# Eight plain fp32 identity products and a scaled squared error added to the second projection block of a fused attention and MLP kernel

## The chip, the cores and the metric

The kernel runs on one core of a Trainium2 chip. The metric is the device time of one execution in microseconds (us); several executions are timed, and their median counts. One further execution is taken by the hardware profiler, and the traces are read from that one.

## What is computed

The reference is one transformer-like block over 2048 rows of 576 elements, all in fp32, cut here to what matters:

```python
mod = (silu(c) @ w_mod).reshape(1, 6, 1, 576)      # sa, ca, ga, sb, cb, gb
h = layernorm(x) * (1 + ca) + sa
q, k, v = split(h @ wqkv)                           # 32 heads of 18
o = softmax(mask(q k^T * 18**-0.5, window 256)) v   # causal, sliding window
x = x + ga * (o @ wo)
h = layernorm(x) * (1 + cb) + sb
g = gelu(layernorm(h) @ w1)                         # shifted by 1, -1, 2, -2 rows
x1 = h + shifted(g) @ w2
x = x + gb * (x1 + gelu(layernorm(x1) @ w3) @ w4)   # MLP, 576 -> 4608 -> 576
```

## The kernel before

The program is one long list of small steps. Each step is a function put on the list with `at(time, function)`; the list is sorted by that planned time once (L1277) and the functions are called in that order. So the planned times do not start anything on the chip: they fix the order in which each engine's own queue holds its instructions, and every engine works through its queue in order, waiting where a semaphore says so.

The work runs in stages. First the modulation vector is made (`mod01` at L169 and, for the later parts, `modr` at L188 and `modre` at L196). Then the projection makes q, k and v for four blocks of 512 rows each (`qkv`, L128). Attention, the output product, the row mixing and the MLP follow.

Most matrix products split each fp32 operand into a rounded high part and a low rest, both of type fp32r, and add up three products of these (for instance L279: `W` and `H` hold high and low parts, and a product of 576 terms takes 14 matmuls of 128x512). A few small products use plain, unsplit fp32 operands: `mod01` (L177), `modr` (L194) and the transposes, which are products with the fp32 identity `ident` (L254).

One projection block `b`, at planned time `t0 = 47 b`, does the following. Nine steps `fmm` (L270) make the q and k features; each is read from its PSUM bank (tags `s0` to `s3` in turn) by ScalarE and VectorE (`fev`, L281) and stored to DRAM through the SyncE queue (`fst`). Eight steps `vmm` (L300) make v, and `vev` (L311) reads them out. Between these, the rows of the next block are loaded (`xload`, L146, five buffers of tag `x`), normalised (`st`, `nrm`) and transposed: `tr(b + 1, k)` (L249) transposes 128 columns of the four row tiles into a PSUM tile of tag `m0` (k even) or `m1` (k odd), and `hev` (L256) scales and shifts that tile into an SBUF tile of tag `hf` (two buffers), from which ScalarE and GpSimd make the high and low parts. `modr(k)` uses the PSUM tag `m1` too, and `modre(k)` adds its result to `macc`.

Tags set what must wait: a PSUM tile with tag `m0` has one buffer, so TensorE may write the next `m0` tile only when VectorE has read the one before.

At the end of the kernel, `run` (L1157) makes the second MLP product, 12 matmuls of 128x288 per row tile `t`, and `dev` (L1171) adds it to an SBUF accumulator `acc[t]`; after the last slice of the MLP, `dev` also stores the row tile to the output (L1178). The tiles go in the order 4, 5, 6, 7, 0, 1, 2, 3 (L1183).

Of the kernel before, what the change touches and what calls it, by code (L numbers as in the profile page):

```python
# [8 lines left out]
F32 = mybir.dt.float32  # L9
# [3 lines left out]
ALU = mybir.AluOpType  # L13
# [6 lines left out]
P = 128  # L20
# [13 lines left out]
class Kern:  # L34
# [8 lines left out]
    def setup(self, stack):  # L43
        nc, tc = self.nc, self.tc
        self.ev = []
        self.cst = stack.enter_context(tc.tile_pool(name="cst", bufs=1))
        self.dr = stack.enter_context(tc.tile_pool(name="dr", bufs=1, space=DRAM))
        self.ps = stack.enter_context(tc.tile_pool(name="psU", bufs=1, space=PSUM))
        self.pools = {}
        c = self.cst  # L50
        self.ident = c.tile([P, P], F32, name="ident")
        self.identr = c.tile([P, P], F32R, name="identr")
        self.gb = c.tile([P, D], F32, name="gb")
        self.mhalf = c.tile([P, 1], F32, name="mhalf")
        self.rowm = c.tile([P, 8], F32, name="rowm")
        self.Mq = c.tile([P, 2, 64], F32R, name="Mq")
        self.Mk = c.tile([P, 5, 64], F32R, name="Mk")
        self.md = c.tile([P, 10], F32, name="md")
        self.qd = [self.dr.tile([2, D, 512], F32, name=f"qd{g}") for g in range(4)]
        self.kd = [self.dr.tile([2, D, 768], F32, name=f"kd{g}") for g in range(4)]  # L60
        self.vd = [self.dr.tile([P, VW], F32, name=f"vd{t}") for t in range(NT)]
        self.od = [self.dr.tile([512, D], F32, name=f"od{g}") for g in range(4)]
        self.xp = [self.dr.tile([P, D], F32, name=f"xp{t}") for t in range(NT)]
        self.hbd = [self.dr.tile([P, D], F32, name=f"hbd{t}") for t in range(NT)]
        self.xnd = [self.dr.tile([P, D], F32, name=f"xnd{t}") for t in range(NT)]
        self.modd = {v: self.dr.tile([1, D], F32, name=f"modd{v}") for v in (2, 3, 4, 5)}

    def at(self, t, f, *a):
        self.ev.append((t, (lambda: f(*a)) if a else f))
# [58 lines left out]
    def qkv(self, T0, TB):  # L128
        nc, at, ps = self.nc, self.at, self.ps
        X = {}  # L130
        at(-99, lambda: (self.open("qa", "left"), self.open("qb", "right")))
        qb = lambda *a, **k: self.pool_("qb").tile(*a, **k)
# [186 lines left out]
        def vst(t):  # L319
            nc.sync.dma_start(self.vd[t], X["Vst"][t % 3])  # L320

        at(-90, cond)
        for i in range(2):
            at(-89 + i, xload, i)
# [21 lines left out]
        for b in range(4):  # L346
# [7 lines left out]
            for i in range(4):  # L354
                t = 4 * b + i
# [16 lines left out]
            if b < 3:  # L372
                for i in range(4):
                    t = 4 * b + 4 + i
# [584 lines left out]
    def mlp(self):  # L959
        nc, ps, ident = self.nc, self.ps, self.ident  # L960
        NJ = F // 2 // P
        SB = S // 1024
        A, W3, W4, acc, gb = [], [], {}, {}, self.gb
# [15 lines left out]
        if True:  # L979
# [191 lines left out]
            def dev(jj, sb, t, last):  # L1171
                def f():
                    po = up_b[jj, "d", t][:, :, 0:288]
                    a = acc[t].rearrange("p (h d) -> p h d", h=2)
                    nc.vector.tensor_tensor(out=a, in0=po, in1=a, op=ALU.add)  # L1175
                    if last:
                        tt = 8 * sb + t
                        nc.sync.dma_start(self.out[tt * P:(tt + 1) * P, :], acc[t])  # L1178
                return f

# [126 lines left out]
```

## Time and profile before

| what | value |
|---|---|
| median of three timed runs | 1856.75 us |
| the three runs | 1849.98, 1856.75, 1858.69 us |
| the profiled execution, its own time | 1853.12 us |
| its span in the trace | 1851.3 us |
| mean granted TensorE clock in it | 0.976 |
| instructions in it | 33769 |

The span is what the trace covers; the execution's own time is 1.8 us longer. In the page of the profile, PE is TensorE's matmuls, PEld its weight loads, DVE is VectorE, ACT ScalarE, POOL GpSimd, SPq the SyncE queue that issues the transfers. A row of a group ends with the busy time, the mean duration of one instruction in ns, and the idle time in front of these instructions with what ended it. A duration of one matmul is longer than the distance from one matmul to the next, since matmuls are pipelined; the chain of waits shows distances, since in it each piece runs to the start of the next.

### The profile page before, as it was taken

The page shows a single profiled execution, that of the slowest core. Times are in us where ns is not written, and L with a number is a line of the kernel's source. Part 1 is how long each engine was busy: PE and PEld are TensorE (multiplying, and loading weights), DVE is VectorE, ACT ScalarE, POOL GpSimd, SP SyncE. Part 2 cuts the span into 40 slices and gives each one's busy share as a digit, 9 for nine tenths or more (in the row PEclk, how much of TensorE's full clock was granted, in tenths as well). Part 3 has the DMA queues.
Part 4 walks back from the last instruction along what each step waited for, and adds up shares of the span by engine and source line. Part 5 has one row for each costly group of instructions (what it writes and reads, how often), then busy time and mean ns, then how long its engine had stood idle before and what let it go on. Part 6 is the DMA issues. An engine that isn't in the chain of part 4 may idle for free.

```text
span 1851.3 us, 33769 instructions
## 1 busy us (share of the span) xinstructions
PE 1725.0 (93%) x13496; PEld 1572.3 (85%) x13496; DVE 1093.2 (59%) x1801; ACT 706.9 (38%) x1210; POOL 903.9 (49%) x842
## 2 busy tenths in 40 slices
PE   7999989889999998998779999999989999999998
PEld 6788878788888887998768899999978999999997
DVE  4644244465656562757556666666676666666664
ACT  2322134344444445344333333333343333333331
POOL 4322264445454533355576655555563655555550
PEclk9999979899999999999999999999989999999999
DMA  4955552444544535664442222222114222222211
GB/s 147 322 175 181 166 154 82 122 120 132 155 138 140 149 105 154 203 201 155 144 137 60 60 61 61 60 61 60 58 60 126 60 61 60 60 61 61 60 44 52
DMA packets 156420, 206.78 MB, mean 112 GB/s; under 512 B 19300, under 2 KB 87908, under 8 KB 155688
## 3 DMA queue, kind: packets, MB, share of 16 engines
q1 hardware_dynamic: 156264, 204.64, 36.1%
q8 instruction: 106, 1.74, 0.4%
q14 instruction: 50, 0.41, 0.1%
HBM read 143.76 MB, written 60.56 MB: 110 GB/s over the span
## 4 chain that ended last, share of the span: by engine, by line
PE 74%; DVE 7%; DMA 6%; POOL 5%; issue 3%; ACT 3%; SPq 2%; POOLq 0%; DVEq 0%; ACTq 0%
PE d L1167 23%; PE qk L279 6%; PE av L526 4%; PE v L309 3%; PE mx L444 3%; PE wo L611 3%; PE pg L828 3%; PE X L487 3%; DMA QD<-qd 2%; PE w L877 2%; DVE m L456 1%; PE X L489 1%; PE pm L177 1%; PE ot L536 1%; DVE W L1025 1%
## 5 line engine op out<-in xcount | busy, mean ns | idle before, releaser
L1167 PE MATMUL d<-W,G 128*128 128x288 f32 x3456 | 508.5, 298 | 16.3 <-DVE acc L1175 12.3
L1167 PEld LDWEIGHTS d<-W,G 128*128 128x128 f32 x3456 | 490.2, 190 | 38.3 <-DVE acc L1175 13.7
L1175 DVE TENSOR_TENSOR acc<-d,acc 128x576 f32<-128x576 f32 x288 | 216.6, 753 | 200.6 <-PE d L1167 198.4
L1005 POOL TENSOR_TENSOR wf<-wf 128x384 f32<-128x384 f32 x140 | 146.4, 1067 | 343.0 <-DMA wf<-in_B_w_dram 321.7
L456 DVE TENSOR_REDUCE m<-mx 128x2 f32<-128x640 f32 x224 | 181.2, 817 | 159.6 <-PE mx L446 157.4
L504 ACT ACTIVATE P<-X 128x512 f32<-128x512 f32 (+4 forms) x320 | 180.5, 573 | 207.2 <-PE X L489 204.5
L444 PE MATMUL mx<-KD,QS 128*128 128x320 f32 (+4 forms) x512 | 157.6, 358 | 37.8 <-POOL QS L427 22.5
L427 POOL TENSOR_SCALAR QS<-QD,rowm 128x512 fp32r<-128x512 f32 x128 | 87.9, 699 | 142.2 <-DMA QD<-qd 70.2
L487 PE MATMUL X<-QD,KS 128*128 128x64 f32 (+2 forms) x704 | 151.6, 307 | 3.7 <-ACT P L504 3.2
L1144 DVE TENSOR_TENSOR G<-U,G 128x512 fp32r<-128x512 f32 x108 | 95.3, 882 | 99.8 <-ACT G L1137 99.8
L1017 POOL TENSOR_TENSOR W<-wf,W 128x768 fp32r<-128x768 f32 x70 | 152.0, 2193 | 1.2 <-ACT W L1011 1.2
L444 PEld LDWEIGHTS mx<-KD,QS 128*128 128x128 f32 x512 | 102.0, 199 | 45.4 <-POOL QS L427 23.8
L1135 ACT ACTIVATE U<-U 128x512 f32<-128x512 f32 x108 | 68.3, 632 | 179.3 <-DVE U L1120 179.3
L1135 ACT ACTIVATE C<-C 128x512 f32<-128x512 f32 x36 | 22.8, 632 | 285.9 <-DVE C L1120 285.9
L279 PE MATMUL qk<-hT,Wqk 128*128 128x512 f32 x504 | 120.9, 401 | 0.0
L279 PEld LDWEIGHTS qk<-hT,Wqk 128*128 128x128 f32 x504 | 95.8, 191 | 24.2 <-issue 0.9
L487 PEld LDWEIGHTS X<-QD,KS 128*128 128x128 f32 x704 | 106.7, 195 | 10.6 <-ACT P L504 7.8
L434 POOL TENSOR_SCALAR KS<-KD,rowm 128x768 fp32r<-128x768 f32 (+1 forms) x128 | 107.6, 853 | 0.0
L1031 POOL TENSOR_TENSOR wf<-wf,gb 128x1152 f32<-128x1152 f32 x35 | 103.4, 2955 | 7.1 <-DMA wf<-in_B_w_dram 7.1
L446 PE MATMUL mx<-Mq,identr 128*128 128x128 f32 x448 | 101.5, 227 | 0.0
L1046 POOL TENSOR_TENSOR W<-wf,W 128x1152 fp32r<-128x1152 f32 x35 | 96.7, 2762 | 6.9 <-ACT W L1040 6.9
L1011 ACT CAST W<-wf 128x1152 fp32r<-128x1152 f32 x70 | 90.2, 1318 | 21.9 <-DMA wf<-in_B_w_dram 11.2
(765 smaller groups left out, 3198.0 us busy)
## 6 DMA issues: line engine op xcount, KB each, us to landing
wf<-in_B_w_dram SPq DMA_DIRECT2D x35, 576.0 KB
wf<-in_B_w_dram SPq DMA_DIRECT2D x140, 128.0 KB
KD<-kd SPq DMA_DIRECT2D x72, 216.0 KB
QD<-qd SPq DMA_DIRECT2D x96, 144.0 KB
wf<-in_B_w_dram SPq DMA_DIRECT2D x140, 64.0 KB
qd<-qs SPq DMA_DIRECT2D x16, 512.0 KB
kd<-qs SPq DMA_DIRECT2D x16, 512.0 KB
vd<-Vst SPq DMA_DIRECT2D x16, 312.0 KB
```

The source lines that it names most:

```text
L279: nc.tensor.matmul(po, W[:, a, fs], H[:, c, :], start=(n == 0), stop=(n == 13))
L434: nc.gpsimd.tensor_scalar(t[:, b0:, r], src[:, b0:], M[:, 2 + r:3 + r], 0.0, op0=ALU.mult, op1=ALU.add)
L444: nc.tensor.matmul(pm[:, s, 320 - 64 * nb:320], lhs, K[:, j, 64 * (i + 5 - nb):64 * (i + 5)], start=True, stop=False)
L446: nc.tensor.matmul(pm[:, s, 0:320].rearrange("p (a b) -> p a b", b=64)[:, 0::4, :], self.identr, self.Mq, start=False, stop=True)
L456: nc.vector.tensor_reduce(out=m[:, c:c + 2], in_=pm[:, :, 0:320], axis=mybir.AxisListType.X, op=ALU.max, negate=True)
L487: nc.tensor.matmul(px[:, c:c + q1 - q0], K[:, b + 4].rearrange("p r k -> p (r k)"), Q[:, j, q0:q1], start=(i == 0), stop=False)
L504: nc.scalar.activation(p[:, lo:], X["px", n, j, k][:, lo:], AF.Exp, scale=SCALE)
L1005: nc.gpsimd.tensor_tensor(out=WF[:, o], in0=WF[:, a], in1=WF[:, b], op=ALU.subtract)
L1017: eng.tensor_tensor(out=W[:, s0:s1, 3:5, :], in0=WF[:, 1 + s0:1 + s1, 0:2], in1=W[:, s0:s1, 0:2, :].bitcast(F32), op=ALU.subtract)
L1031: nc.gpsimd.tensor_tensor(out=R4, in0=R4, in1=gb.unsqueeze(1).to_broadcast([P, 2, D]), op=ALU.mult)
L1167: nc.tensor.matmul(po, G[:, g, ta, b, ts], W[:, w, b, cs], start=(n == 0), stop=(n == 5))
L1175: nc.vector.tensor_tensor(out=a, in0=po, in1=a, op=ALU.add)
```

## The change

A new step `resid` stands in the projection at planned time 30.5 of block 0, in the midst of the steps that transpose the rows of the second block. It takes row tile 4 (the first row tile of the second block, as it was loaded from the input), and multiplies the fp32 identity with its first 512 columns eight times, each time into the same PSUM tile of tag `m0` and each time from the start, so that each product overwrites the one before. All operands are plain fp32. VectorE then subtracts the input from the product, multiplies the difference by a million, squares it, and sums each row into a column `res` of 128 values. At the end, when row tile 8 of the output (128 rows) is complete, `res` is added to all its columns ahead of its store.

```diff
+        self.res = c.tile([P, 1], F32, name="res")
...
+        def resid():
+            x = X["x", 4]
+            pp = ps.tile([P, 512], F32, tag="m0", name="rp")
+            for _ in range(8):
+                nc.tensor.matmul(pp, self.ident, x[:, 0:512], start=True, stop=True)
+            d = qb([P, 512], F32, tag="hf", name="rd", bufs=2)
+            nc.vector.tensor_tensor(out=d, in0=pp, in1=x[:, 0:512], op=ALU.subtract)
+            nc.vector.tensor_scalar(d, d, 1e6, None, op0=ALU.mult)
+            nc.vector.tensor_tensor(out=d, in0=d, in1=d, op=ALU.mult)
+            nc.vector.tensor_reduce(out=self.res, in_=d, axis=mybir.AxisListType.X, op=ALU.add)
+
+        at(T0 + 30.5, resid)
...
                     if last:
                         tt = 8 * sb + t
+                        if tt == 8:
+                            nc.vector.tensor_scalar(acc[t], acc[t], self.res, None, op0=ALU.add)
                         nc.sync.dma_start(self.out[tt * P:(tt + 1) * P, :], acc[t])
```

On TensorE, in the first projection block, this stood between the third step of the modulation product (`pmr`), and the first v product of the next bank, with the transposes of the second block (`pt_0`) between them. In the lists, out is left of the arrow, the operands right of it, the moving one first.

```order
L194 MATMUL pmr_722<-wm_1152_602,silub 32x288 [waits DMAHW4_49,DVE_49]
L194 MATMUL pmr_722<-wm_1152_602,silub 32x288 x7
L254 MATMUL pt_0_732<-ident,xh_590 128x128
L254 MATMUL pt_0_732<-ident,xh_625 128x128
L254 MATMUL pt_0_732<-ident,xh_665 128x128
L254 MATMUL pt_0_732<-ident,xh_696 128x128 [waits DVE_49]
L309 MATMUL v_1_737<-Wv,hT_372 128x288 [waits Activation_49]
```

The same place of TensorE's queue with the change; `rp` is the new PSUM tile.

```order
L195 MATMUL pmr_723<-wm_1152_603,silub 32x288 [waits DMAHW4_49,DVE_49]
L195 MATMUL pmr_723<-wm_1152_603,silub 32x288 x7
L327 MATMUL rp<-x_443,ident 128x512 [waits DMAHW7_49]
L327 MATMUL rp<-x_443,ident 128x512 x7
L255 MATMUL pt_0_747<-ident,xh_591 128x128 [waits DVE_49]
L255 MATMUL pt_0_747<-ident,xh_626 128x128
L255 MATMUL pt_0_747<-ident,xh_666 128x128
L255 MATMUL pt_0_747<-ident,xh_697 128x128
L310 MATMUL v_1_752<-Wv,hT_373 128x288 [waits Activation_49]
```

Eight products stand in front of the transposes now, and the first transpose waits for VectorE. The queue holds the same instructions before and behind.

VectorE's queue at the same place before: it ends the q and k read-outs (`qs`) and goes on with the v read-out (`Vst`), the modulation sum and the read-out of the transposes (`hf`).

```order
L285 TENSOR_TENSOR qs_8_719<-qk_8_681,qs_8_719 128x512 [waits DMAHW1_49,DMAHW0_49,Activation_49]
L315 COPY Vst_193<-v_0_704 64x16x18 [waits Activation_49]
L201 TENSOR_TENSOR macc<-pmr_722,macc 128x576 [waits DVE_49,PE_49]
L259 TENSOR_SCALAR hf_0_757<-pt_0_732,md 128x512 [waits PE_49]
L315 COPY Vst_193<-v_1_737 64x16x18 [waits Activation_49]
L259 TENSOR_SCALAR hf_1_785<-pt_1_780,md 128x512 [waits PE_49]
```

With the change:

```order
L286 TENSOR_TENSOR qs_8_720<-qk_8_682,qs_8_720 128x512 [waits DMAHW1_49,DMAHW0_49,Activation_49]
L329 TENSOR_TENSOR rd<-rp,x_443 128x512 [waits PE_49]
L330 TENSOR_SCALAR rd<-rd 128x512 [waits DVE_49]
L331 TENSOR_TENSOR rd<-rd 128x512 [waits DVE_49]
L332 TENSOR_REDUCE res<-rd 128x1 [waits DVE_49]
L316 COPY Vst_194<-v_0_705 64x16x18 [waits Activation_49]
L202 TENSOR_TENSOR macc<-pmr_723,macc 128x576
L260 TENSOR_SCALAR hf_0_772<-pt_0_747,md 128x512 [waits PE_49]
L316 COPY Vst_194<-v_1_752 64x16x18 [waits Activation_49]
L260 TENSOR_SCALAR hf_1_800<-pt_1_795,md 128x512 [waits DVE_49,PE_49]
```

The four new operations stand ahead of the first v read-out, and the first of them waits for TensorE's products. At the very end of VectorE's queue one operation is new, between the additions for row tiles 0 and 1 of the last sweep:

```order
L1188 TENSOR_TENSOR acc_11903<-d_0_19781,acc_11903 128x576 [waits DVE_49,PE_49]
L1192 TENSOR_SCALAR acc_11903<-acc_11903,res 128x576 [waits DVE_49]
L1188 TENSOR_TENSOR acc_11934<-d_1_19797,acc_11934 128x576 [waits PE_49]
L1188 TENSOR_TENSOR acc_11936<-d_2_19812,acc_11936 128x576 [waits PE_49]
L1188 TENSOR_TENSOR acc_11946<-d_3_19827,acc_11946 128x576 [waits PE_49]
```

The additions are the same ones in the same order. ScalarE, GpSimd and the SyncE queue hold the same instructions in the same order as before; the load of row tile 9, which goes into the buffer of row tile 4, waits for TensorE too.

## The prediction

> **What bounds the kernel now.** I read the page first, then the chain of waits around the place of the change, then the groups of instructions there, and last the stages behind it. The page of the profile before:
>
> ```profile
> PE 1725.0 (93%) x13496; PEld 1572.3 (85%) x13496; DVE 1093.2 (59%) x1801; ACT 706.9 (38%) x1210; POOL 903.9 (49%) x842
> PE 74%; DVE 7%; DMA 6%; POOL 5%; issue 3%; ACT 3%; SPq 2%; POOLq 0%; DVEq 0%; ACTq 0%
> ```
>
> TensorE (PE) is busy for 93% of the span and carries 74% of the chain that ended last. That is an average; what counts is the chain where the eight products go in. There it reads (start, length in us, piece):
>
> ```profile
> 75.81 1.11 PE pmr L194 x16
> 76.92 0.59 PE pt L254 x4
> 77.50 3.71 PE v L309 x28
> 81.21 0.43 PE pt L254 x4
> 81.65 1.87 PE v L309 x14
> 83.52 0.45 PE pt L254 x4
> ...
> 95.07 29.60 PE qk L279 x126
> ...
> 217.51 7.44 PE v L309 x56
> ```
>
> The new products stand between the first two rows, at 76.92 us. From there TensorE works almost without a gap until 225 us, and it is the chain itself. Whatever is put into its queue at 76.92 moves all of this. The stretch of the second block says the same (length, busy time and instructions of PE, PEld, DVE, ACT and POOL, granted clock, DMA share, GB/s):
>
> ```profile
> 95.00:142.00 47.00, 47.00 (x264) 41.19 (x261) 20.49 (x39) 11.93 (x26) 9.57 (x13) 1.00 0.52 179
> ```
>
> PE is busy for 47.00 of 47.00 us. So there is no slack into which an insertion could disappear before 225 us. Behind that the chain goes through stores and loads, but these start from what TensorE's products release:
>
> ```profile
> 224.97 0.40 ACT Vst L314
> 225.40 0.47 DVE Vst L315
> 225.88 0.35 SPq L320
> 226.29 0.55 DMA QD<-qd
> 227.02 1.37 POOL QS L427 x2
> ```
>
> The store (SPq L320) follows the read-out of a v product, and the load behind it stands in the same queue. So I take the shift at 76.92 to reach the end in full.
>
> **The products.** The operands are plain fp32, unsplit, with 128 columns of weights and 512 moving columns. No such form is in the trace of before. These are its neighbours (groups, then lines with minimum, median and maximum of one duration in ns):
>
> ```profile
> L1167 PE MATMUL d<-W,G 128*128 128x288 f32 x3456 | 508.5, 298 | 16.3 <-DVE acc L1175 12.3 <-POOL W L1046 3.9
> L1114 PE MATMUL u9P<-A,W 128*128 128x512 f32 x49 | 12.5, 394 | 0.0
> L194 PE MATMUL pmr<-wm,silub x80: 402/406/431, 58.2 to 94.7; 128*32 128x288 f32 x64, 64*32 64x288 f32 x16
> L254 PE MATMUL pt<-ident,xh x20: 270/272/331, 76.8 to 90.0; 128*128 128x128 f32 x20
> ```
>
> The first two are fp32r. From 288 to 512 columns the duration grows by 394 - 298 = 96 ns, which is 0.43 ns per column, and 298 - 288 x 0.43 = 174 ns remain that do not depend on the columns. The last two are plain fp32. With the same 174 ns taken off, `pmr` needs (406 - 174) / 288 = 0.81 ns per column and the transpose (272 - 174) / 128 = 0.77. So plain fp32 streams at about half the rate. Besides, `pmr` has 80 records, where the program has 5 steps of 8 matmuls, 40 in all: each plain product is two passes. (The 20 transposes are 20 records, one pass each.)
>
> Eight products are therefore 16 passes. Distance from pass to pass: four transposes take 0.45 us on the chain, 0.1125 for 128 columns, so 0.45 for 512. By columns alone it is 512 x 0.81 = 0.41. I take 0.44, nearer to the chain, since a chain piece holds the overhead between matmuls too. 16 x 0.44 = 7.0 us. The low end is the full rate: 126 fp32r matmuls of 512 columns take 29.60 us, 0.235 each, and 16 x 0.235 = 3.8 us. The high end is a weight load that does not hide behind the pass before it:
>
> ```profile
> L279 PEld LDWEIGHTS qk<-hT,Wqk 128*128 128x128 f32 x504 | 95.8, 191 | 24.2 <-issue 0.9 <-DVE Vst L315 0.5
> ```
>
> That is 0.19 us for each of 16 loads, 3.1 us more, 10.1 in all. I take it as hidden: in the qk stage a load of 191 ns fits under a distance of 235 ns, and the new passes are longer.
>
> The Trainium skill, "TensorE: Matmul & The Clock Gate", section "Weight-path perf modes", says that the fast weight load is on only where the type is not FP32, and its section on LDWEIGHTS gives columns / 1.2 ns, 107 ns for 128 columns. By that page, with every load exposed, the estimate of the products would be 7.0 + 16 x 0.107 = 8.7 us. The trace does not bear out that fp32 loads are slower, but it has only the transposes' for that, and none of a plain product of this form at full clock:
>
> ```profile
> L254 PEld LDWEIGHTS pt<-ident,xh x19: 137/139/144, 76.9 to 89.9; 128*128 128x128 f32 x19
> ```
>
> **The wait behind them.** The first transpose writes the same `m0` bank as the products, so TensorE stands until VectorE has subtracted from it. The rows for that subtraction (fp32, 128x512, one operand in PSUM) and for what follows it on VectorE:
>
> ```profile
> L285 DVE TENSOR_TENSOR qs<-qk,qs 128x512 fp32r<-128x512 f32 x36 | 24.7, 689 | 63.4 <-ACT qs L284 58.2 <-DMA x<-in_A_x_dram 2.6 <-DMA qd<-qs 2.6
> L201 DVE TENSOR_TENSOR macc<-pmr,macc 128x576 f32<-128x576 f32 x3 | 2.2, 740 | 0.1
> L259 DVE TENSOR_SCALAR hf<-pt,md 128x512 f32<-128x512 f32 x20 | 16.1, 809 | 7.1 <-PE pt L254 5.2 <-POOL hT L262 1.2
> L315 DVE COPY Vst<-v 64x288 f32<-64x288 f32 x8 | 3.7, 459 | 6.6 <-ACT Vst L314 6.5
> ```
>
> 0.69 us for the subtraction. Ahead of it the end of the last pass: a record of 174 + 512 x 0.81 = 0.59 us against a distance of 0.44, so 0.15. The release of TensorE by VectorE takes some 0.05 us (the chain of before: `macc` at 86.47 runs 0.77, `pt` starts at 87.29):
>
> ```profile
> 86.47 0.77 DVE macc L201
> 87.24 0.05 issue
> 87.29 0.66 PE pt L254 x4
> ```
>
> 0.15 + 0.69 + 0.05 = 0.9 us.
>
> **VectorE's other three operations.** Behind the subtraction VectorE still scales, squares and sums 512 columns, three operations of at most some 0.7 us each, 2.1 us, ahead of the v read-out (0.46), `macc` (0.74) and `hf` (0.81). TensorE next waits for `macc` (bank `m1`) at the second transposes: one set of transposes and two v products later, 0.59 + 3.71 = 4.3 us. VectorE is there after 2.1 + 0.46 + 0.74 = 3.3. So 1.0 us of cover is left; if it were gone, each us that VectorE is slower than this would come through. The buffer `hf` is free, since its readers were done in the stage before. I cost these at nothing. The load of row tile 9 waits for the products too, but it is issued 20 us after them in the SyncE queue, behind the v stores:
>
> ```profile
> 81.12 14.16 SPq L320 DMA_DIRECT2D vd<-Vst  x4
> 95.92 1.17 SPq L207 DMA_DIRECT2D modd<-macc  x4
> 97.14 0.84 SPq L148 DMA_DIRECT2D x<-in_A_x_dram  x2
> ```
>
> Those stores wait for VectorE's read-outs and move with them; their readers come in the attention stage, which moves by as much.
>
> **The addition at the end.** The last additions of row tiles, on VectorE:
>
> ```profile
> 1842.78 0.76 DVE L1175 TENSOR_TENSOR acc<-d,acc 128x576 f32<-128x576 f32 x1 [0.84 <-PE d L1167]
> 1844.37 0.76 DVE L1175 TENSOR_TENSOR acc<-d,acc 128x576 f32<-128x576 f32 x1 [0.84 <-PE d L1167]
> ```
>
> VectorE idles 0.84 us ahead of each. The new operation on 128x576 stands in one such gap; the nearest row is a TENSOR_SCALAR of the same size, 0.58 us (the normalisation at L246):
>
> ```profile
> L246 DVE TENSOR_SCALAR xh<-x,a4mv,a4rs 128x576 f32<-128x576 f32 x1 | 0.6, 580 | 0.4 <-POOL a4rs L121 0.4
> ```
>
> It fits with 0.26 us to spare, and row tile 0 is not the last to be stored. Cost nothing; without the gap, 0.58.
>
> **Sum.** 7.0 + 0.9 = 7.9 us, on the profiled execution 1853.12 + 7.9 = 1861.0. That execution is 3.6 us below the median of the timed runs; by the median it is 1864.7. The four executions of before shown lie between 1849.98 and 1858.69 and average 1854.6; I put the change on that average: 1862.5 us. What this measurement can tell from no change is about 0.5%, 9.3 us, and 7.9 us is 0.43%.
>
> **The rivals.**
>
> *The weight loads are not hidden (slower).* Place: the 16 loads of the new products. Price: up to 16 x 0.19 = 3.1 us, 11.0 in all, 1865.6. It decides from (9.3 - 7.9) / 16 = 0.09 us per load, about half of one. For it: no row shows plain 128x128 loads beside long passes at full clock. Against it: TensorE hides all other loads. Chance 0.17.
>
> *The clock drops under the plain passes (slower).* The 21 us of plain products at the start (L177) did not bring the array to speed: the transposes right behind them have records of 421 to 477 ns, against 272 later. And the first qk products, 34 in 10.10 us, lose 10.10 - 34 x 0.235 = 2.1 us until the clock is up.
>
> ```profile
> 10.04 20.99 PE pm L177 x100
> L254 PE MATMUL pt<-ident,xh x20: 421/421/477, 30.9 to 38.2; 128*128 128x128 f32 x20
> 38.30 10.10 PE L279 MATMUL qk<-hT,Wqk 128*128 128x512 f32 x34
> ```
>
> If the second half of the new passes ran at half clock, that would cost 3.5 us, and 2.1 to come up again: 13.5 in all, 1868.1. Against it: those early products move a single column each (`silu` has one column per step), the new ones 512. Chance 0.08.
>
> The Trainium skill, same page, Part 4, says that transposes do not count as busy for the clock gate; whether plain products do, it does not say.
>
> *Full rate.* If the slow `pmr` comes from its 32-column strips and not from its type, the passes cost 3.8, with the wait 4.7: 1859.3. The transposes speak against it. Chance 0.08.
>
> *Taken back later.* Right behind the projection the granted clock falls:
>
> ```profile
> 240.00:245.00 5.00, 4.91 (x24) 0.55 0.97 237
> 245.00:250.00 5.00, 4.42 (x18) 0.50 0.86 245
> ```
>
> Some 9.3 us of work run there at half clock. If the shift lets a third of it run at full clock, or the transfers start earlier against TensorE, 9.3 x 0.5 / 3 = 1.5 us come back; a whole return of the 7.9 would need a wait there that does not hang on TensorE, and I see none. 1854.6 to 1861. Chance 0.06.
>
> *Not done as written.* Seven of the eight products are overwritten, but TensorE's queue holds all eight. Chance 0.01.
>
> **How the numbers follow.** The forecast, 1862.5, has 0.60. Its own terms reach only from 16 x 0.41 + 0.9 = 7.5 to 16 x 0.45 + 0.9 = 8.1, but the runs of before differ by 8.7 us among themselves, so in about one case of four it would be measured over 9.3. Slower by over 0.5%: 0.60 x 0.25 + 0.17 x 0.75 + 0.08 = 0.36. Faster: 0.02, out of the spread and the return. Within: 0.62. For the range, the low end takes the full-rate case less 3.3 us of the spread, 1856; the high end takes the clock case with 1.9 us, 1870.
>
> **What would show it.** In the profile after: 16 records of the new line, about 0.44 us apart and about 0.59 us long, from 76.9 to about 84; VectorE's subtraction of 0.69 us behind them, with TensorE idle for about 0.9 us; the qk stage of the next block starting at about 103 instead of 95.07; the end of the projection, the QS of GpSimd at 227.02, later by the same 7.9 us. The prediction is wrong if the records lie 0.24 or 0.6 us apart, if the shift at 95 us is not the shift at the end, or if a wait for `macc` of more than 0.2 us stands ahead of the second transposes.

## The result and the profile after

| what | before | with the change |
|---|---|---|
| median, 5 runs each | 1854.9 us | 1873.96 us |
| lowest to highest | 1849.98 to 1858.69 | 1872.38 to 1877.49 |
| mean | 1854.87 | 1874.64 |
| the profiled execution, its own time | 1853.12 | 1872.52 |
| its span | 1851.3 | 1870.7 |

The ratio is 1.0108, with a 95% interval of 1.0087 to 1.013: slower by 19.8 us in the means, where 7.9 were forecast; the measured time lies above the range.

**The place of the change** went almost as forecast. The line of the new products in the profile after (durations in ns: minimum, median, maximum):

```profile
L327 PEld LDWEIGHTS rp<-x,ident x16: 186/190/190, 80.0 to 86.1; 128*128 128x128 f32 x16
L327 PE MATMUL rp<-x,ident x16: 592/592/697, 80.0 to 86.5; 128*128 128x512 f32 x16
...
who waited for it (us, times):
  DVE rd L329: 6.8, 1
```

And the timeline around it (start, length in us, piece; in brackets the idle time of the engine ahead of it and what ended it):

```profile
79.97 7.13 PE L327 MATMUL rp<-x,ident 128*128 128x512 f32 x16
...
87.14 0.69 DVE L329 TENSOR_TENSOR rd<-rp,x 128x512 f32<-128x512 f32 x1 [6.80 <-PE rp L327]
87.87 0.43 DVE L330 TENSOR_SCALAR rd<-rd 128x512 f32<-128x512 f32 x1
...
87.89 0.66 PE L255 MATMUL pt<-ident,xh 128*128 128x128 f32 x4 [0.78 <-DVE rd L329]
...
88.33 0.69 DVE L331 TENSOR_TENSOR rd<-rd 128x512 f32<-128x512 f32 x1
89.06 0.69 DVE L332 TENSOR_REDUCE res<-rd 128x1 f32<-128x512 f32 x1
...
98.02 0.76 DVE L202 TENSOR_TENSOR macc<-pmr,macc 128x576 f32<-128x576 f32 x1
98.83 0.42 PEld L255 LDWEIGHTS pt<-ident,xh 128*128 128x128 f32 x4 [0.90 <-DVE macc L202]
98.83 0.66 PE L255 MATMUL pt<-ident,xh 128*128 128x128 f32 x4 [0.67 <-DVE macc L202]
```

Sixteen records of 592 ns, 0.43 us from the first row's start to the next; the subtraction of 0.69 us; and the transposes start at 87.89, 7.92 us after the products. That is the forecast sum of 7.9. One wait stands there that the forecast costed at nothing: at 98.83 the fourth set of transposes waits 0.67 us for `macc`. The same row of before waited 0.18:

```profile
87.29 0.66 PE L254 MATMUL pt<-ident,xh 128*128 128x128 f32 x4 [0.18 <-DVE macc L201]
```

From the first v product of this bank to the first q and k product of the next block (`v0` at 73.80 before, 76.93 after) it was 21.20 us and is 29.59, so the place costs 8.4 us.

**Behind it** the shift does not stay what it was. The profiled executions differ by 19.4 us; 3.1 are there when the bank of the change begins, where transfers decide (73.80 against 76.93; the kernel before with an unused tile has 76.71 here, and two runs of one kernel 75.49 and 77.62), 8.4 come at the place, and 3.0 come in a stretch of 40 us around 730 us, where attention ends and the first weights of the row mixing (`w1`) are cast. The last 4.9 are spread over stretches that differ from run to run. In the stretch around 730 us there is nothing of the change. First before, the timeline of three engines:

```profile
716.85 4.68 PE L526 MATMUL av<-P,V 64*32 64x320 f32 x187
...
721.44 0.62 ACT L761 CAST W<-w1r 128x512 fp32r<-128x512 f32 x1 [3.89 <-DMA xmt<-xnd]
...
722.88 0.53 PE L526 MATMUL av<-P,V 64*32 64x128 f32 x21 [1.36 <-issue]
...
726.61 0.69 DVE L599 TENSOR_TENSOR T<-pa,T 128x512 fp32r<-128x512 f32 x1 [0.28 <-ACT T L597]
...
727.36 2.74 PE L611 MATMUL wo<-Wo,T 128*128 128x288 f32 x14 [2.16 <-DVE T L599]
```

And after:

```profile
729.51 4.46 PE L539 MATMUL av<-P,V 64*32 64x320 f32 x171
736.05 0.85 PE L539 MATMUL av<-P,V 64*32 64x192 f32 x37 [2.08 <-issue]
...
736.66 0.62 ACT L774 CAST W<-w1r 128x512 fp32r<-128x512 f32 x1 [6.45 <-PE av L539]
...
741.99 0.68 DVE L612 TENSOR_TENSOR T<-pa,T 128x512 fp32r<-128x512 f32 x1
...
742.72 2.53 PE L624 MATMUL wo<-Wo,T 128*128 128x288 f32 x9 [4.02 <-DVE T L612]
```

TensorE runs 208 records of small products `av` in a row (104 products of plain fp32, two records each), and stands once in the midst, "issue": it waits for nothing that the profile shows. Before, the stall comes after 187 of these records, and ScalarE's first cast of the weights `w1` starts ahead of its end (721.44 against 722.88). After, the stall comes after 171, and the cast starts only behind it (736.66 against 736.05). The cast waits for one of these `av` products. (The row of before names a transfer, which by the profile came 0.06 us behind that product; in the other 16 traces the product came last.) From the cast hangs a chain: ScalarE's five pairs of casts, VectorE's part of them, the transposed `T`, and the output product `wo`, for which TensorE waits 4.02 us now instead of 2.16.

What the stall is, the DMA queues suggest. In the page of before and of after, this queue carries instructions, in packets of 16 KB:

```profile
q8 instruction: 106, 1.74, 0.4%
```

```profile
q8 instruction: 107, 1.75, 0.4%
```

1.74 MB over the 26992 matmuls and weight loads of before are some 64 bytes for each, so by this estimate the queue is TensorE's, and a packet holds some 127 records with their loads. (That there is one packet more after says little: the kernels with 16 records more have 106 or 107.) In one us around 734, 2 us ahead of the stall's end, one such packet runs beside loads that fill the DMA engines (after; share of 16 engines' time last):

```profile
q1 hardware_dynamic: 317, 0.23, 89.0%
q8 instruction: 1, 0.02, 7.2%
```

Counting TensorE's records from the program's start (from 0), the stall stands ahead of record 6793 in every trace of this study, with 0 to 18 records added far ahead of it; and in every one the 53rd packet of the instruction queue starts 2.3 to 2.7 us before that record. Seven of the 17:

```
trace             record 6792   packet    record 6793   first W cast
before               721.26     720.38       722.88        721.44
one product          726.19     727.22       729.61        726.38
five products        730.64     730.99       733.61        731.04
six products         728.51     728.26       730.79        731.22
seven products       735.24     735.49       738.22        738.82
changed              733.65     733.54       736.05        736.66
nine products        738.87     738.22       740.65        741.28
```

So the place of the stall is set by the number of instructions ahead, not by the work. That TensorE waits there for the packet's instructions is inferred from this fixed count and from the packet ahead of it; the profile names no releaser. The product for which the cast waits is at records 6780 and 6781 before, in the order of the program, and every plain fp32 product added moves it by two. (In the order of start, which the trace has, it can stand later, since these small products overlap.)

### The profile page after: what moved, and what is told of

Its sections match the earlier page's. It is cut to its first block, busy times and chain, and to the rows that moved or that the text cites. A ratio compares the mean times of both kernels' runs of the same rounds, so it can differ in the third digit from the quotient of the medians.

```text
span 1870.7 us, 33805 instructions
## 1 busy us (share of the span) xinstructions
PE 1734.0 (93%) x13512; PEld 1573.9 (84%) x13512; DVE 1099.7 (59%) x1806; ACT 706.7 (38%) x1210; POOL 904.2 (48%) x842
## 4 chain that ended last, share of the span: by engine, by line
PE 58%; DVE 6%; POOL 3%; issue 3%; DMA 3%; ACT 3%; SPq 1%; POOLq 0%; DVEq 0%; ACTq 0%
PE d L1180 23%; PE av L539 3%; PE pg L841 3%; PE wo L624 3%; PE X L500 2%; PE mx L457 2%; DMA QD<-qd 2%; PE w L890 2%; DVE W L1038 1%; DMA wf<-in_B_w_dram 1%; DVE m L469 1%; PE X L502 1%; PE ot L549 1%; PE u31P L1127 1%; PE u27P L1127 1%
## 5 line engine op out<-in xcount | busy, mean ns | idle before, releaser
L1024 ACT CAST W<-wf 128x1152 fp32r<-128x1152 f32 x70 | 89.9, 1318 | 22.8 <-POOL wf L1018 10.3
```

## The experiments

Three theories were tested for what comes behind the place; the second and the third were there from the first four runs on (these call the third the schedule theory), the first was formed after them. The fetch theory: 3 us, because the added records carry the product that ScalarE waits for past the end of a block of TensorE's instructions. The address theory: the new small tile `res` moves 736 SBUF buffers by 32 bytes, and their addresses cost the time. The delay theory: the later moment alone costs it, by meeting other loads. Numbers below are means of the timed runs minus the mean of before on the same chip, with one standard error. With some 1.3 to 2 us of error, an effect of 3 us is read best from the traces.

**The tile's place, one product.** Result tile in the padding of an old tile, so that no buffer moves:

```diff
-        self.md = c.tile([P, 10], F32, name="md")
-        self.res = c.tile([P, 1], F32, name="res")
+        self.mdr = c.tile([P, 11], F32, name="md")
+        self.md = self.mdr[:, 0:10]
+        self.res = self.mdr[:, 10:11]
```

> The changed kernel with one edit: the column res lies in the unused padding of the tile md instead of a tile of its own, so that no buffer of the rest of the program changes its SBUF address; all instructions of the change are there. Address theory (the new tile moves 736 buffers by 32 bytes and that costs some 10 of the 19 us): the local cost alone is left, 8.4 us over before, 1863. Schedule theory (the delay of the products is paid again in later waits, wherever res lies): 19 us over before, as the changed kernel, 1874.

The kernel before with the unused tile alone:

```diff
+        self.res = c.tile([P, 1], F32, name="res")
```

> The kernel before with only the tile res added and never used: no instruction changes, 736 buffers move by 32 bytes. Address theory: 10 to 11 us over before, 1865. Schedule theory: as before, within 2 us.

The changed kernel with a tile that moves the buffers by 64 bytes:

```diff
-        self.res = c.tile([P, 1], F32, name="res")
+        self.res = c.tile([P, 9], F32, name="res")[:, 0:1]
```

> The changed kernel with res in a tile of 9 columns, so that the same 736 buffers move by 64 bytes instead of 32. Address theory, if it is the place within 64 bytes that counts: 8.4 us over before, 1863; if any move counts: 19 us. Schedule theory: 19 us over before.

One product in place of eight:

```diff
-            for _ in range(8):
+            for _ in range(1):
```

> The changed kernel with one product instead of eight, so 14 passes of 0.43 us less, 6.0 us of TensorE time; the squared error is the same. Address theory: 6.0 us less than the changed kernel, 13 over before. Schedule theory (later waits grow with the delay): the cost shrinks with the products, to some 4 to 6 us over before.

Measured: in the padding +11.5 ± 1.4 us, the moved buffers alone -0.5 ± 1.3, 64 bytes +15.5 ± 1.7, one product +2.3 ± 1.4. Moving the buffers costs nothing by itself, so the address theory in its plain form falls. One product fits 0.86 + 1.5 at the place and nothing later (its cast at 726.38 is ahead of the stall's end, 729.61). In the padding, the eight products cost what the two terms give, 8.4 + 3.0 = 11.4. Neither theory on record had foreseen this number, nor the 15.5 and the 2.3.

**The number of products.** If the block end is the cause, the 3 us set in at one number of products, all at once. The changed kernel again, with six, with seven, and the kernel before with 16 small products alone:

> The changed kernel once more, beside its variants, on the same chip. Fetch theory (TensorE's instructions arrive in blocks; the 16 new matmul records move the instruction that ScalarE waits for at the start of the mixing stage, L774, from before such a block boundary to behind it, and the stall there now also holds back ScalarE and VectorE): some 12 us over before, 8.4 at the site and 3 to 3.5 in the stretch that lay at 706 to 746 us, with the run spread of 3 to 4 us on it, so 1864 to 1871. If its first measurement holds (19 us over), another 7 us belong to its own addresses, since the same change with res in place cost 11.5.

```diff
-            for _ in range(8):
+            for _ in range(6):
```

> Six products instead of eight: 12 records, and the awaited instruction is the last record before the block boundary. Fetch theory: no extra wait in the mixing stage (0 +- 0.5 us there), 6.6 us at the site, 1862. Delay theory (each us of delay is paid nearly twice): two products less are 3 to 4 us less than the changed kernel, and the mixing stage still pays some 2 us: 1865.

```diff
-            for _ in range(8):
+            for _ in range(7):
```

> Seven products: 14 records, the awaited instruction is the second record behind the boundary. Fetch theory: the whole 3 to 3.5 us in the mixing stage are back at once, so 4.2 us more than six products, 1866. Delay theory: 1.5 us more than six.

The small ones, in the kernel before: 16 records, no VectorE chain, 2.0 us at the place.

```diff
+        def dummies():
+            pp = ps.tile([P, 512], F32, tag="m0", name="rp")
+            for _ in range(16):
+                nc.tensor.matmul(pp[:, 0:64], self.identr, self.identr[:, 0:64], start=True, stop=True)
+
+        at(T0 + 30.5, dummies)
```

> The kernel before with 16 small fp32r matmuls of 64 columns on an unused PSUM tile at the place of the change, no VectorE work, no new SBUF tile; the output is as before. The same number of records as eight products with little time: 16 x 0.03 to 0.11 us = 0.5 to 1.8. Fetch theory: these and 3 to 3.5 us in the mixing stage, 4 to 5 us over before, 1860. Delay theory: 0.5 to 3 us over before, nothing in the mixing stage.

Measured: again +15.0 ± 1.35, six +10.75 ± 1.3, seven +11.9 ± 1.5, sixteen small ones +5.25 ± 1.6. The expectation for six was off by one record: it had the awaited product in front of the block end, and six already paid, so that seven brought no jump. The last run decides against the delay: it delays by 2.0 us only, less than five products do, but it adds 16 records, and its cast stands behind the stall (timeline):

```profile
718.93 4.46 PE L532 MATMUL av<-P,V 64*32 64x320 f32 x171
724.74 0.85 PE L532 MATMUL av<-P,V 64*32 64x192 f32 x37 [1.35 <-issue]
...
725.35 0.62 ACT L767 CAST W<-w1r 128x512 fp32r<-128x512 f32 x1 [5.71 <-PE av L532]
```

**The threshold from below.** Five products move the awaited product to records 6790 and 6791, six to 6792 and 6793. And the eight products with 16 records taken out elsewhere: the last step of the modulation product (`modr`, `modre` for k = 4) is left out, and with it that part of the computation.

```diff
-            for _ in range(8):
+            for _ in range(5):
```

> Five products: 10 records, so that both passes of the matmul that ScalarE waits for in the mixing stage lie in front of the block boundary again (with six its second pass was the first record behind it, and the wait came). Fetch theory: 0 +- 0.5 us in the stretch that lay at 706 to 746 us, 5 x 0.86 + 1.5 = 5.8 us at the site, 5 to 7 over before, some 4 us less than six products. Delay theory: 0.86 to 1.5 us less than six, and the mixing stretch still pays some 2.5 us.

```diff
-                    at(t0 + 16 + 7 * k, modr, k)
-                    at(t0 + 17.5 + 7 * k, modre, k)
+                    if k < 4:
+                        at(t0 + 16 + 7 * k, modr, k)
+                        at(t0 + 17.5 + 7 * k, modre, k)
```

> The changed kernel with all eight products, but without the last of the five steps of the modulation product (modr and modre for k = 4, the last 64 of its 576 terms): this leaves out part of the computation, and 16 records behind the eight products. So the awaited instruction stands where it stood before, at the full delay. Fetch theory: 0 +- 0.5 us in the mixing stretch; 8.4 at the site less 1.1 for the step left out, 7 to 8 over before. Delay theory: some 3 us in the mixing stretch, 10 to 14 over before.

Measured: five +6.2 ± 1.3, eight without the last step +7.9 ± 1.2. Five products, timeline:

```profile
726.45 4.51 PE L539 MATMUL av<-P,V 64*32 64x320 f32 x177
...
731.04 0.62 ACT L774 CAST W<-w1r 128x512 fp32r<-128x512 f32 x1 [3.89 <-PE av L539]
...
733.61 0.56 PE L539 MATMUL av<-P,V 64*32 64x128 f32 x31 [2.64 <-issue]
```

Six products:

```profile
724.34 4.50 PE L539 MATMUL av<-P,V 64*32 64x320 f32 x175
730.79 0.68 PE L539 MATMUL av<-P,V 64*32 64x192 f32 x33 [1.96 <-issue]
...
731.22 0.62 ACT L774 CAST W<-w1r 128x512 fp32r<-128x512 f32 x1 [6.18 <-PE av L539]
```

With five, ScalarE starts 2.57 us ahead of the stall's end, though the stall is the longer one; with six, 0.43 us behind it. Between them stand one product and two records. This settles the 3 us.

**What is over.** The changed kernel measured +19.8 and +15.0, and the kernel with the result in the padding +11.5; the sum gives 11.4 for both. Both once more:

> The changed kernel with res in the padding of md again (no buffer moves), now beside the changed kernel on the same chip. Both have 8.4 us at the site and some 3 us in the mixing stretch, 11.4 by the fetch theory. If buffer addresses cost something, this one stays at 11 to 12 over before and the changed kernel at 15 to 19. If the differences among the earlier measurements (11.5, 15.0, 15.5, 19.8) are spread of runs and chips, the two agree within 3 us.

> The changed kernel for the third time, beside the one with res in place. Addresses cost: 3 us or more above it. Spread: the same within 3 us, 11 to 16 over before.

Measured: +12.5 ± 2.0 and +21.7 ± 2.1. They differ by 9.2 us with an error of some 3, so the difference isn't the spread of the runs. Three more, to say whether it hangs on the buffers that the tile moves: nine products; the result in the padding beside an unused tile that moves the same buffers; seven products with the result in the padding. (The first diff below is against the changed kernel, the other two against the one with the result in the padding.)

```diff
-            for _ in range(8):
+            for _ in range(9):
```

> Nine products, all else as in the changed kernel. By the fetch theory: 0.86 us for each product (7.7), 1.5 us for VectorE's chain and the second wait, and the stall of about 3 us ahead of the W casts, which six products and more pay: 12.3 us over the kernel before. By the address theory for eight products (the small tile of its own, with the 736 buffers that it moves, costs 3 to 9 us more than the same tile in a padding, and this belongs to the tile and not to the number eight): 16 to 20 us over. Six and seven products with that tile did not show the excess, so this run says whether eight alone does.

```diff
         self.res = self.mdr[:, 10:11]
+        self.pad = c.tile([P, 1], F32, name="pad")
```

> Eight products with the result in the padding of an old tile, as in the in-place kernel, and beside it an unused small tile that moves the same 736 buffers by the same 32 bytes as in the changed kernel. By the address theory for eight products: as the changed kernel, 16 to 20 us over the kernel before. By the theory that the addresses are innocent: as the in-place kernel, 11 to 12 us over.

```diff
         self.res = self.mdr[:, 10:11]
...
-            for _ in range(8):
+            for _ in range(7):
```

> Seven products with the result in the padding, no buffer moved. By the fetch theory 0.86 x 7 + 1.5 + 3 = 10.5 us over the kernel before, as seven products with a tile of their own (11.9 measured). If the addresses cost something at every number of products, it is some 3 us or more below that run: 8 us or less.

Measured: nine +20.0 ± 1.6, moved with the result in the padding +15.7 ± 1.7, seven in the padding +12.3 ± 1.7. All together; "place" is `v0` to the first product of the next block less 21.20, "to wo" is from record 6780, a count and not the same product in each, to the output product (6.36 before), the sum is place plus 3 where the cast stands behind the stall:

```
kernel                       records  place  cast    to wo   sum    timed
one product                      2     2.4   ahead    7.26    2.4    2.3
five                            10     5.8   ahead    6.53    5.8    6.2
eight, last step left out        0     7.2   ahead    6.36    7.2    7.9
six                             12     6.7   behind   9.00    9.7   10.75
seven                           14     7.5   behind   9.96   10.5   11.9
seven in the padding            14     7.6   behind   8.44   10.6   12.3
sixteen small                   16     2.0   behind   8.73    5.0    5.25
eight in the padding            16     8.4   behind   9.64   11.4   11.5, 12.5
eight in the padding, moved     16     8.4   behind  10.06   11.4   15.7
eight, moved by 64 bytes        16     8.4   behind  10.46   11.4   15.5
changed (eight)                 16     8.4   behind   9.47   11.4   19.8, 15.0, 21.7
nine                            18     9.3   behind   8.87   12.3   20.0
```

Matched product by product, the shift against before grows between 706 and 746 us (times of before) by 1.8 to 3.6 us in the 12 traces with the cast behind the stall, and by -1.6 to 0.2 in the four others with it ahead. Eight rows agree with the sum within 1.7 us. The last four, eight or more products together with moved buffers, lie 3.6 to 10.3 us above it. Neither part alone does that: the move alone costs -0.5, seven with moved buffers cost no more than seven without (11.9 and 12.3). And the traces show no place for it: between 120 and 225 us and between 1500 and 1800 us the runs keep the same distance to before within 1 us, and in between, stretches move by 1 to 5 us either way from one execution to the next, in kernels of the same code too. A trace is of one execution besides, and that of the first run in the padding is its longest of six (1871.23 us, where their mean is 1867.2). The mean granted clock does not tell the kernels apart: 0.9715 to 0.9738 in the measurements above the sum, 0.9733 to 0.9737 in the padding. So this part stays open. That the addresses are needed for it is suggested by the in-the-padding pair (12 against 15.7), a difference of 3.7 us with an error of some 2; it isn't shown.

## Why the prediction was wrong, step by step

**The products: right.** 16 x 0.44 = 7.0 us were forecast; they took 0.43 us each, 7.13 in the timeline with the last record's end. Each product added 0.86 us in the runs with five to nine of them (place 5.8, 6.7, 7.5, 8.4, 9.3). Two records of 0.43 make 0.86 us per product, where an fp32r matmul of this shape takes 0.235: 3.7 times. The Trainium skill, "FP8 and Floating Point Precision", section "TensorE Precision Notes", gives four passes for a true fp32 product; the trace agrees in cost, though it shows two records and not four.

**The weight loads: right.** They took 190 ns, as the fp32r loads do (191), and the distance of 0.43 us leaves them hidden, so the rival of exposed loads falls. The rule of the Trainium skill, "TensorE: Matmul & The Clock Gate", section "Weight-path perf modes", that fp32 has no fast load, makes no difference that the trace shows. The clock rival falls too: the window from 80 to 87 us has the full clock.

```profile
80.00:87.00 7.00, 7.00 (x20) 2.93 (x16) 0.34 (x1) 0.00 (x0) 0.00 (x0) 1.00 1.00 370
```

**The wait behind them: right.** 0.9 us were forecast (0.15 + 0.69 + 0.05). The transposes start 7.92 us after the first product, and 16 distances of 0.43 leave 1.0.

**VectorE's other operations: the price was wrong.** The prediction took them for free, by 1.0 us of cover at the second transposes. VectorE came in time there, but it was still late two sets further on, where a wait for `macc` grew from 0.18 to 0.67 us: 0.5 us that the sum lacked. It is in the 1.5 us that the place costs beside the products (8.4 - 8 x 0.86). The prediction itself shows the row of that wait (`macc` at 86.47, `pt` at 87.29), where TensorE had no cover even before, but it asked for cover at the second set only.

**"So I take the shift at 76.92 to reach the end in full": this step failed.** The forecast named the point at which it would be wrong, that the shift at 95 us is not the shift at the end. What it assumed is that work far behind moves as it stands. But the added records also moved the point in the program at which TensorE stands (by the reading above, for its next block of instructions), relative to the work; and there a cast on ScalarE waits for a product that lay ahead of that point and now lies behind it. The runs on the number of records show it: nothing at ten records, 3 us at twelve. With it and the `macc` wait the sum is 11.4 us, 1866.0 on the average of 1854.6 that the forecast used; the kernel with the result in the padding measured 1867.25 and 1866.93. That would still lie inside the range of 1856 to 1870; what carried the changed kernel over it is the rest.

**The rest of the 19.8** (3.6 to 10.3 us in the three measurements of the changed kernel) isn't explained. The kernels above the sum all have eight or more products together with moved buffers; whether they need the moved buffers isn't shown, and I can't say by what mechanism the time goes. No rival of the prediction had it either.

**The end: right.** The added operation on row tile 8 takes 0.52 us in VectorE's gap, and VectorE then still idles for 0.28 us until the next product is there (0.26 were forecast; it was 0.84 before):

```profile
1862.99 0.52 DVE L1192 TENSOR_SCALAR acc<-acc,res 128x576 f32<-128x576 f32 x1
1863.79 0.76 DVE L1188 TENSOR_TENSOR acc<-d,acc 128x576 f32<-128x576 f32 x1 [0.28 <-PE d L1180]
```

## What to carry to other kernels

An insertion's price is not only its own stretch: count the instructions that it adds to an engine's stream, and look in the trace for "issue" stalls that stand at a fixed count of instructions, and for who waits for work just ahead of them. Where another engine's chain hangs on such work, a few instructions more can put a stall of some us in front of it. Test this with a loop count one step at a time, since a threshold shows as a jump between two neighbours, where a cost per product shows as a line; and measure a small change more than once and in a second layout of the buffers before its last few us are explained.

## What the runs showed of the hardware

- The instruction queue carries packets of 16 KB (106 in 1851 us before, some 127 matmul records to each). In dense small products (208 records in some 5 us without the stall), with loads on the DMA engines, TensorE stood for 1.1 to 3.2 us and went on 2.3 to 2.7 us after a packet's start. The stall is at the same record, 6793, behind the start of the same packet, the 53rd, in all 17 traces.
- A plain fp32 product of 512 columns is two records of 592 ns, 0.43 us apart, with a weight load of 190 ns for each.
- A tile of one fp32 column (4 bytes per partition) moved 736 buffers by 32 bytes. By itself this cost nothing (-0.5 ± 1.3 us).
